# A long convolution joined with a two-layer MLP: token tiles of 512 columns in place of 390, a reordered second stage, and moved loads

## The chip, the cores and the metric

The kernel runs on one core of a Trainium2 chip. The metric is device time in microseconds (us) of one launch. The engines of the core are called PE (TensorE, with its weight loads as PEld), DVE (VectorE), ACT (ScalarE), POOL (GpSimd) and SP (SyncE, which here only issues DMAs).

## The reference

Two batches of 12480 tokens with 128 channels. The first part is a causal convolution of length 12480 by Fourier transforms, the second a two-layer MLP on each token:

```python
h_filt = (np.maximum(pos_emb @ w1, 0.0) @ w2) * window       # 12480 x 128
u = x * v                                                     # 2 x 12480 x 128
y = irfft(rfft(u, 2S) * rfft(h_filt, 2S))[:, :S]
t = (x * y).reshape(24960, 128)
h = t @ w_in                                                  # 128 -> 2048
out = np.maximum(0.01 * h, h) @ w_out                         # 2048 -> 128
```

## The kernel before

**The transform.** The convolution is a transform of length 98 x 128 in two stages. Stage 1 multiplies 98-row blocks by cosine tables (`ft`, `f1`) and stores to a scratch array in DRAM, stage 2 works on 25 chunks (`NCH`) of four rows `k` of that array: forward in 128 points, product with the spectrum of the filter, back in 128 points, store to `scr2`. A last stage (`front`) goes back over 98 points for one pair of column blocks at a time, `yp` (16 matmuls), and multiplies by `x`.

**Batch 0** does stage 1 and stage 2 ahead of the MLP, to about 350 us. The loop over its 25 chunks also makes the filter's spectrum and splits the MLP's weights. `load_b(c + 2)` fetches a chunk two turns ahead. In its last turn `load_tile(0)` issues, on SP's queue, the table `g` (300 KB), the tokens `xm` (192 KB and two small ones) and `cin` (the output of stage 2) of the first pair.

**The MLP** runs over 64 tiles, one for each pair, of `TOK` = 390 columns, and in each over 16 blocks `f` of the hidden layer (a step is one `f` of one tile). All operands are split into a high and a low part in fp32r, so a product is three matmuls. `m1(t, f)` is three matmuls into a PSUM tile `mh`; ACT makes `rh = relu(mh)` (L697), DVE makes `rl = relu(mh) - rh` (L698). `m2` of the step three before then adds three matmuls to `acc`; for f = 0 three more go first (L707 to L709). So a tile takes 16 x 6 + 3 = 99 matmuls of 390 columns. Between the steps the program emits, in an order written out by hand:

- `finish(t - 1)` at f = 2, 5, 7: copy of `acc`, four transposes into `op`, copy, store to the output;
- `join(t + 1)` at f = 6: two operations on POOL from `cin` to `cp`;
- `front(t + 1)` at f = 9 (transposes of `xm` into `xp`) and f = 12 (`yp`, then on DVE `zf`, on ACT `zh`, on POOL `zl`);
- the transform of batch 1, `conv1`, a generator cut into pieces at its yields. 32 pieces (`AHEAD`) go ahead of the MLP; the others are spread evenly, `(pieces - AHEAD) * slots // (SLOTS - 28)`, over the steps of batch 0, from the second step on.

In `conv1` stage 1 has 16 turns of 8 pieces. A turn fetches the next one's table and tokens (`fetch_a`, 600 KB and twice 384 KB), and POOL multiplies x by v (`mult_a`, L177). `fetch_a(4)` is issued in the turn c = 3 of the generator, within the 32 pieces, and once more by the line ahead of the MLP's loop (L744), into other buffers that nothing reads. Stage 2 (`conv1b`) takes about 15 pieces for a chunk: three-term products `up` (L131, 512 columns), `us` and `p1` on ACT, DVE and POOL, the back product `dp` of the chunk before and its copies, `ph` and `pl`, then `split` of the next chunk (`th` on ACT, `tl` on DVE L393).

Each engine works its instructions in program order. Each DMA queue issues in order, and an issue that waits holds those behind it.

Of the kernel before, what the change touches and what calls it, by code (L numbers as in the profile page):

```python
# [23 lines left out]
TOK = 4 * NA - 2  # L24


@with_exitstack
def tile_conv_mlp(ctx, tc, x, v, pos_emb, w1, w2, w_in, w_out, cf, cr, cg, cb, ci, cw, out):
# [128 lines left out]
    with tc.manual_schedule():  # L157
# [172 lines left out]
        N1 = HB // MC1  # L330
        PRE = 3
# [35 lines left out]
        def conv1b():  # L367
# [4 lines left out]
            def fetch_b(c):  # L372
                k0, n = chunk(c)
                t = pool.tile([128, KC, 2, D], F32, tag="bin1", name="bin1")
                nc.sync.dma_start(out=t[:, :n].rearrange("p k s d -> p k (s d)"), in_=scr1b[:, k0:k0 + n, :])
# [4 lines left out]
                got[c] = t  # L380
# [17 lines left out]
            for _ in range(5):  # L398
                yield
            yield from split(0)  # L400
            late, pins = None, {}
            for c in range(NCH + 1):
                if c + 1 < NCH:
                    fetch_b(c + 1)
# [3 lines left out]
                if c < NCH:  # L408
                    n = chunk(c)[1]
                    w = n * D  # L410
                    h, (th, tl) = hd.pop(c), parts.pop(c)
                    yield
                    up = psc["next"]()
                    for s in range(2):
                        three(up[s][:, :w].rearrange("p (k d) -> p k d", d=D), (mb_h[:, s], mb_l[:, s]),
                              (th[:, :n, s, :], tl[:, :n, s, :]))
                    yield

                    us = pool.tile([128, 2, 512], F32, tag="us", name="us", bufs=1)
                    p1 = pool.tile([128, 2, 512], F32, tag="p1", name="p1", bufs=1)  # L420
# [26 lines left out]
                if c + 1 < NCH:  # L447
                    yield from split(c + 1)
# [3 lines left out]
        pieces = N1 * (MC1 // 2) * 4 + 20 + 14 * NCH  # L452
# [7 lines left out]
        def load_tile(t):  # L460
# [8 lines left out]
            nc.sync.dma_start(out=xt[ROWS:, 0], in_=x[b, None, r0:r0 + 2, :])  # L469
            ci_t = mlp.tile([NA, 2, 2, 2, D], F32, tag="cin", name="cin")  # L470
# [3 lines left out]
            ld[t] = (ci_t, g, xt)  # L474
# [12 lines left out]
        with ExitStack() as st:  # L487
# [162 lines left out]
            evac(NCH - 1)  # L650
            ahead(A2)
# [11 lines left out]
        COLS = [(1, 0, 0, NA - 1), (1, 1, NA - 1, NA - 1), (0, 0, 2 * NA - 2, NA), (0, 1, 3 * NA - 2, NA)]  # L663

        def front(t):
# [15 lines left out]
            zh = sm.tile([128, TOK], F32R, tag="zh", name="zh")  # L681
            zl = sm.tile([128, TOK], F32R, tag="zl", name="zl")
            nc.vector.tensor_tensor(out=zf, in0=yp, in1=xs, op=ALU.mult)  # L683
            nc.scalar.copy(zh, zf)  # L684
            (nc.gpsimd if t else nc.vector).tensor_tensor(out=zl, in0=zf, in1=zh, op=ALU.subtract)  # L685
            z[t] = (zh, zl)

        def m1(t, f):
            zh, zl = z[t]
            hp = ps.tile([128, TOK], F32, tag="mh", name="mh", bufs=3)  # L690
# [4 lines left out]
            rh = sm.tile([128, TOK], F32R, tag="rh", name="rh", bufs=5)  # L695
            rl = sm.tile([128, TOK], F32R, tag="rl", name="rl", bufs=5)
# [4 lines left out]
        def m2(t, f, r):  # L701
            rh, rl = r
            if f == 0:
                zh, zl = z[t]
                ap = ps.tile([128, TOK], F32, tag="acc", name="acc", bufs=2)
                acc[t] = ap
# [3 lines left out]
            ap = acc[t]  # L710
# [4 lines left out]
        def finish(t):  # L715
            b, mp = divmod(t, NT)
            ot = sm.tile([128, TOK], F32, tag="ot", name="ot")
            nc.scalar.copy(ot, acc.pop(t))
            yield
            op = ps.tile([NA, 4, D], F32, tag="io", name="op")  # L720
            for p, m, at, n in COLS:
                nc.tensor.transpose(op[:, 2 * p + m, :], ot[:, at:at + NA], ident)  # L722
            os_ = sm.tile([NA, 2, 2, D], F32, tag="os", name="os")
            nc.scalar.copy(os_.rearrange("a p m d -> a (p m) d"), op)
            yield
            n = b * S
            dst = out[n:n + ROWS * NB, :].rearrange("(a p n) d -> a p n d", p=2, n=HB)
            for r in (slice(0, R0), slice(R0, ROWS)):
                nc.sync.dma_start(out=dst[r, :, 2 * mp:2 * mp + 2, :], in_=os_[r])
            r0 = n + ROWS * NB + 2 * mp  # L730
            nc.sync.dma_start(out=out[None, r0:r0 + 2, :], in_=os_[ROWS:, 0])

        total = B * NT
        SLOTS = NT * NF
        slots, done = 0, AHEAD
# [8 lines left out]
        fetch_a(4)  # L744
        pend = []
        fin = iter(())
        for t in range(total):
            if t + 1 < total and (t + 1) % NT:
                load_tile(t + 1)
            for f in range(NF):  # L750
                pend.append((t, f, m1(t, f)))
                if len(pend) > 3:
                    m2(*pend.pop(0))
                if f == 2 and t:
                    fin = finish(t - 1)
                if f in (2, 5, 7):
                    next(fin, None)
                if t + 1 == NT and f == 6:
                    run(conv)
                    load_tile(t + 1)  # L760
                if t + 1 < total:
                    if f == 6 and (t + 1) % NT:
                        join(t + 1)
                    if f == 9:
                        if (t + 1) % NT == 0:
                            join(t + 1)
                        frt = front(t + 1)
                    if f in (9, 12):
                        next(frt, None)
                if t < NT:  # L770
                    slots += 1
                    while done < AHEAD + (pieces - AHEAD) * slots // (SLOTS - 28):
# [4 lines left out]
        run(finish(total - 1))  # L777
# [68 lines left out]
```

## Time and profile before

| | us |
|---|---|
| median of 3 runs | 1787.03 |
| lowest, highest | 1785.88, 1787.2 |
| the profiled execution | 1786.13 |
| its span, first to last instruction | 1784.3 |
| PE busy in the span | 1709.8 |
| DVE, ACT, POOL busy | 952.3, 893.2, 559.3 |

The profile is one execution; its time and the median are 0.9 us apart. Busy time of PE counts overlapping matmuls once, and their ends are modelled, so how fast PE goes is read from the starts of matmuls, not from its busy share.

### The profile page before, as it was taken

Reading aid. Unit: us, or ns where it says so; the run is one execution under the profiler, and the core shown is the slowest. Engines: PE = TensorE matmul, PEld = TensorE weight load, DVE = VectorE, ACT = ScalarE, POOL = GpSimd, SP = SyncE. Lnnn points to the kernel's source line nnn. Section 1 sums busy time; section 2 is a strip of 40 time slices with the busy share of each in tenths; the row PEclk is TensorE's granted clock in tenths of the full one; section 3 lists DMA queues with packets and bytes.
Section 4 is the critical chain, followed back from the end, with each engine's and each line's share of the span. In section 5 each row is a group of like instructions: output and inputs, shape, how many; then the busy total and the mean of one; then the engine's idle time right before and its main releaser. Section 6 shows DMA issues by size and latency. Waiting matters only on the chain.

```text
span 1784.3 us, 29254 instructions
## 1 busy us (share of the span) xinstructions
PE 1709.8 (96%) x10620; PEld 1608.9 (90%) x10620; DVE 952.3 (53%) x1711; ACT 893.2 (50%) x1803; POOL 559.3 (31%) x427
## 2 busy tenths in 40 slices
PE   6788999889999999999999999999999999999998
PEld 5677555579999999999999999999999999999998
DVE  3566788744555555555555554444444444444444
ACT  1222444424445666666666666444444444444444
POOL 3453222122323555555544554211111112111120
PEclk8889999989999999999999999999999999999999
DMA  9898999796766465555555542222111221112210
GB/s 225 240 267 255 329 333 343 238 248 192 202 169 175 130 171 142 133 138 134 141 143 145 145 127 72 59 59 67 51 51 51 62 64 51 51 50 66 61 51 15
DMA packets 147708, 251.78 MB, mean 141 GB/s; under 512 B 10842, under 2 KB 96742, under 8 KB 144492
## 3 DMA queue, kind: packets, MB, share of 16 engines
q1 hardware_dynamic: 127420, 224.21, 45.3%
q10 hardware_dynamic: 20144, 25.69, 4.1%
q8 instruction: 84, 1.38, 0.3%
q14 instruction: 60, 0.49, 0.1%
HBM read 166.37 MB, written 83.43 MB: 140 GB/s over the span
## 4 chain that ended last, share of the span: by engine, by line
PE 79%; DMA 10%; DVE 6%; SPq 2%; issue 1%; ACT 1%; POOL 1%; ACTq 0%; POOLq 0%; DVEq 0%
PE mh L692 10%; PE mh L694 10%; PE acc L712 10%; PE acc L711 10%; PE mh L693 10%; PE acc L713 10%; PE yp L678 6%; PE cv L131 4%; PE cv L349 2%; DMA scr<-o 2%; DMA ft<-in_cf_dram 2%; PE op L722 2%; PE xp L670 1%; DVE ta L125 1%; PE up L117 1%
## 5 line engine op out<-in xcount | busy, mean ns | idle before, releaser
L698 DVE SCALAR_TENSOR_TENSOR rl<-mh,rh 128x390 fp32r<-128x390 f32 x1024 | 574.9, 564 | 616.6 <-ACT rh L697 614.8
L697 ACT ACTIVATE rh<-mh 128x390 fp32r<-128x390 f32 x1024 | 508.5, 498 | 386.9 <-PE mh L694 369.9
L692 PE MATMUL mh<-zh,w_in_h 128*128 128x390 f32 x1024 | 365.5, 357 | 0.0
L694 PE MATMUL mh<-zh,w_in_l 128*128 128x390 f32 x1024 | 349.9, 342 | 0.0
L693 PE MATMUL mh<-zl,w_in_h 128*128 128x390 f32 x1024 | 348.9, 341 | 0.0
L712 PE MATMUL acc<-rl,w_out_h 128*128 128x390 f32 x1024 | 348.4, 340 | 0.0
L711 PE MATMUL acc<-rh,w_out_h 128*128 128x390 f32 x1024 | 348.0, 340 | 0.0
L713 PE MATMUL acc<-rh,w_out_l 128*128 128x390 f32 x1024 | 347.8, 340 | 0.0
L685 POOL TENSOR_TENSOR zl<-zf,zh 128x390 fp32r<-128x390 f32 x63 | 65.0, 1032 | 706.3 <-ACT zh L684 699.0
L692 PEld LDWEIGHTS mh<-zh,w_in_h 128*128 128x128 f32 x1024 | 193.9, 189 | 2.2 <-DVE rl L698 0.2
L693 PEld LDWEIGHTS mh<-zl,w_in_h 128*128 128x128 f32 x1024 | 193.6, 189 | 2.1
L712 PEld LDWEIGHTS acc<-rl,w_out_h 128*128 128x128 f32 x1024 | 193.8, 189 | 0.0
L694 PEld LDWEIGHTS mh<-zh,w_in_l 128*128 128x128 f32 x1024 | 193.8, 189 | 0.0
L713 PEld LDWEIGHTS acc<-rh,w_out_l 128*128 128x128 f32 x1024 | 193.0, 188 | 0.0
L711 PEld LDWEIGHTS acc<-rh,w_out_h 128*128 128x128 f32 x1024 | 192.7, 188 | 0.0
L678 PEld LDWEIGHTS yp<-g,cp 98*128 98x128 f32 x1024 | 123.5, 192 | 0.5 <-issue 0.5
L678 PE MATMUL yp<-g,cp 98*128 98x97 f32 (+1 forms) x1024 | 123.2, 273 | 0.3 <-issue 0.3
L430 POOL TENSOR_TENSOR us<-us,hd 128x512 f32<-128x512 f32 (+1 forms) x50 | 63.6, 1273 | 145.8 <-ACT us L428 145.8
L684 ACT CAST zh<-zf 128x390 fp32r<-128x390 f32 x64 | 33.2, 519 | 149.3 <-DVE zf L683 149.3
L484 POOL TENSOR_TENSOR cp<-cin 98x512 f32<-98x512 f32 x63 | 88.3, 1402 | 0.0
L98 ACT COPY a1s<-a 98x384 f32<-98x384 f32 x64 | 30.7, 480 | 112.8 <-PE a L313 57.4
L483 POOL TENSOR_TENSOR cp<-cin 98x512 f32<-98x512 f32 x63 | 81.5, 1293 | 17.9 <-DMA cin<-scr 10.6
(127 smaller groups left out, 2102.1 us busy)
## 6 DMA issues: line engine op xcount, KB each, us to landing
cin<-scr SPq DMA_DIRECT2D x63, 392.0 KB
hd<-hspec SPq DMA_DIRECT2D x48, 512.0 KB
g<-in_cg_dram SPq DMA_DIRECT2D x64, 300.1 KB
scr<-o SPq DMA_DIRECT2D x32, 588.0 KB
bin<-scr SPq DMA_DIRECT2D x23, 768.0 KB
scr1b<-o SPq DMA_DIRECT2D x32, 392.0 KB
hspec<-hs ACTq DMA_DIRECT2D x48, 256.0 KB
scr<-ct ACTq DMA_DIRECT2D x24, 512.0 KB
```

Of the source, the lines that this page charges most:

```text
L131: nc.tensor.matmul(dst, u, w, start=(i == 0), stop=(i == 2))
L483: eng.tensor_tensor(out=o1, in0=c0, in1=c1, op=ALU.subtract)
L484: eng.tensor_tensor(out=o0, in0=c0, in1=c1, op=ALU.add)
L678: nc.tensor.matmul(yp[:, at:at + n], ci_t[:, r, m, p, :], g[:, r, p, m, :n], start=(r == 0), stop=(r == 1))
L692: nc.tensor.matmul(hp, w_in_h[:, fs], zh, start=True, stop=False)
L693: nc.tensor.matmul(hp, w_in_h[:, fs], zl, start=False, stop=False)
L694: nc.tensor.matmul(hp, w_in_l[:, fs], zh, start=False, stop=True)
L697: nc.scalar.activation(out=rh, in_=hp, func=AF.Relu)
L698: nc.vector.scalar_tensor_tensor(out=rl, in0=hp, scalar=0.0, in1=rh, op0=ALU.max, op1=ALU.subtract)
L711: nc.tensor.matmul(ap, w_out_h[:, f, :], rh, start=False, stop=False)
L712: nc.tensor.matmul(ap, w_out_h[:, f, :], rl, start=False, stop=False)
L713: nc.tensor.matmul(ap, w_out_l[:, f, :], rh, start=False, stop=(f == NF - 1))
```

## The change

The MLP runs over 50 tiles instead of 64: the first has 390 columns, then 23 of 512 and one of 314 end batch 0; batch 1 has 23 of 512 and two of 352. The pairs stay as they are (64 of 390 columns), so a pair's `zh`, `zl` and its output are written in up to two pieces (111 in all instead of 64), by `pieces_of`. `zh` and `zl` have three buffers instead of two, `rh` and `rl` four instead of five, and `m2` follows `m1` by two steps instead of three (`DEEP`). A table of steps (`ends`, `steps`) says when the front, join and load of each pair are emitted: the front's second half at least three steps ahead of the tile that needs it, join seven steps before that.

The pieces of batch 1's transform are paced by `pace`: none in the first 14 steps, stage 1 up to step 120, then stage 2 up to six steps ahead of step 375. In stage 2 `split` of the next chunk stands ahead of the back product, its load one chunk sooner, `us` and `p1` have two buffers, and 12 pieces instead of 5 lie between the first load and its use. `load_tile` is cut in `load_gx` and `load_c`: the g and x of pairs 0 and 1 are loaded in the turns of chunks 20 and 21, `cin` of pair 1 behind the last chunk. The second `fetch_a(4)` goes. (Pair 33's load is now issued twice, at steps 375 and 383.)

```diff
+        WAIT = 12
             fetch_b(0)
-            for _ in range(5):
+            fetch_h(0)
+            fetch_b(1)
+            for _ in range(WAIT):
                 yield
...
+                if c + 1 < NCH:
+                    yield from split(c + 1)
+                    fetch_b(c + 2)
                 if c:
                     wb = chunk(c - 1)[1] * D
...
-                if c + 1 < NCH:
-                    yield from split(c + 1)
...
+                if c in (NCH - 5, NCH - 4):
+                    load_gx(c - NCH + 5)
                 if c == NCH - 1:
-                    load_tile(0)
+                    load_c(0)
...
             evac(NCH - 1)
+            load_c(1)
             ahead(A2)
...
+        rest = S - TOK - (S - TOK) // WIDE * WIDE
+        widths = [TOK] + [WIDE] * ((S - TOK) // WIDE) + [rest]
+        left = S - (S // WIDE - 1) * WIDE
+        widths += [WIDE] * (S // WIDE - 1) + [left - left // 2, left // 2]
...
+            for k, a, c, n in pieces_of(t):
+                if k not in z:
+                    z[k] = [sm.tile([128, WIDE], F32R, tag=g, name=g, bufs=ZB) for g in ("zh", "zl")]
+                zh, zl = (i[:, a:a + n] for i in z[k])
+                nc.scalar.copy(zh, zf[:, c:c + n])
+                (nc.gpsimd if t else nc.vector).tensor_tensor(out=zl, in0=zf[:, c:c + n], in1=zh, op=ALU.subtract)
...
+        ZB, DEEP = 3, 2
+        first = [next(pieces_of(t))[0] for t in range(total)]
+        ends, e = {}, NTL * NF
+        for t in reversed(range(1, total)):
+            e = min(e - 8, first[t] * NF - 3)
+            ends[t] = e
...
+            at(ends[t] - 7, "join", t)
+            at(ends[t] - 3, "front", t)
+            at(ends[t], "front", t)
+            if t % NT == 0:
+                at(ends[t] - 14, "conv", t)
...
-        fetch_a(4)
+        STAGE1 = N1 * (MC1 // 2) * 4
+        FROM, TILL = 14, 120
+        def pace(i):
+            if i < TILL:
+                return AHEAD + (STAGE1 - AHEAD) * max(0, i - FROM) // (TILL - FROM)
+            return STAGE1 + (pieces - STAGE1) * (i + 1 - TILL) // (SLOTS - 6 - TILL)
...
-        for t in range(total):
+        for k in range(NTL):
             for f in range(NF):
-                if len(pend) > 3:
+                if len(pend) > DEEP:
                     m2(*pend.pop(0))
+                for s_ in steps.get(i, ()):
+                    do(*s_)
```

## Rows read from the trace of the kernel before

**Rows 1.** Windows: stretch, length, busy us (instructions) by engine, clock, DMA share, GB/s

```profile
360.00:391.00 31.00, 22.14 (x120) 21.35 (x119) 9.71 (x19) 8.71 (x17) 7.12 (x4) 0.83 0.90 249
...
575.00:1100.00 525.00, 524.32 (x3069) 507.91 (x3068) 283.20 (x478) 342.79 (x687) 267.03 (x211) 1.00 0.52 137
1100.00:1784.30 684.30, 679.45 (x4127) 675.98 (x4125) 322.22 (x570) 333.16 (x676) 115.64 (x99) 1.00 0.20 55
```

**Rows 2.** Groups by line: shapes, count, busy us, mean ns, idle before

```profile
L698 DVE SCALAR_TENSOR_TENSOR rl<-mh,rh 128x390 fp32r<-128x390 f32 x1024 | 574.9, 564 | 616.6 <-ACT rh L697 614.8
L697 ACT ACTIVATE rh<-mh 128x390 fp32r<-128x390 f32 x1024 | 508.5, 498 | 386.9 <-PE mh L694 369.9 <-ACT th L388 0.4
...
L426 DVE TENSOR_TENSOR p<-cv,hd 128x512 f32<-128x512 f32 (+1 forms) x50 | 34.1, 681 | 16.9 <-ACT us L425 13.3 <-DMA xm<-in_x_dram 1.0
```

**Rows 3.** Timeline of PE around 905 us: start us, length us, instruction

```profile
901.95 0.35 PE L692 MATMUL mh<-zh,w_in_h 128*128 128x390 f32 x1
...
907.30 0.33 PE L692 MATMUL mh<-zh,w_in_h 128*128 128x390 f32 x1
...
908.88 0.39 PE L131 MATMUL cv<-th,mb_h 128*128 128x512 f32 x1
...
910.25 0.34 PE L692 MATMUL mh<-zh,w_in_h 128*128 128x390 f32 x1
```

**Rows 4.** The chain that ended last, one of its six-matmul pieces: start, us

```profile
885.94 1.39 PE cv L131 x6
```

**Rows 5.** Timeline of PE where the MLP begins; in brackets idle before, and releaser

```profile
358.13 1.91 PE L349 MATMUL cv<-xv,ft 98*98 98x128 f32 x16
359.80 0.42 PE L692 MATMUL mh<-zh,w_in_h 128*128 128x390 f32 x1
...
366.31 3.13 PE L349 MATMUL cv<-xv,ft 98*98 98x128 f32 x16 [4.52 <-POOL xv L177]
369.10 0.68 PE L692 MATMUL mh<-zh,w_in_h 128*128 128x390 f32 x1
...
385.45 3.73 PE L349 MATMUL cv<-xv,ft 98*98 98x128 f32 x16 [4.34 <-POOL xv L177]
388.83 0.68 PE L692 MATMUL mh<-zh,w_in_h 128*128 128x390 f32 x1
```

**Rows 6.** Timeline of POOL over the same stretch

```profile
363.92 2.34 POOL L177 TENSOR_TENSOR xv<-xv,xv 98x1024 f32<-98x1024 f32 x1 [32.85 <-DMA xv<-in_v_dram]
...
385.35 1.26 POOL L483 TENSOR_TENSOR cp<-cin 98x512 f32<-98x512 f32 x1
```

**Rows 7.** Timeline of SP's queue, 290 to 400 us

```profile
314.51 0.34 SPq L495 DMA_DIRECT2D bin<-scr  x1
...
335.98 0.69 SPq L472 DMA_DIRECT2D cin<-scr  x1
...
362.54 0.33 SPq L164 DMA_DIRECT2D ft<-in_cf_dram  x1
```

**Rows 8.** Timeline of ACT's queue: stores of stage 2 of batch 0

```profile
333.05 0.37 ACTq L147 DMA_DIRECT2D scr<-ct  x1
...
348.92 0.37 ACTq L147 DMA_DIRECT2D scr<-ct  x1
```

**Rows 9.** Timeline of PE near the end of batch 0's chunks

```profile
323.76 1.04 PE L580 MATMUL ep<-mb,bin 128*64 128x128 f32 x16
```

**Rows 10.** Timeline of PE, batch 1's second stage: the last matmul of an `m1`

```profile
906.59 0.33 PE L694 MATMUL mh<-zh,w_in_l 128*128 128x390 f32 x1
```

**Rows 11.** Timeline of DVE, the same stretch

```profile
909.21 1.02 DVE L698 SCALAR_TENSOR_TENSOR rl<-mh,rh 128x390 fp32r<-128x390 f32 x2
```

**Rows 12.** Timeline of PE at a tile's end in batch 1's MLP

```profile
1511.10 1.92 PE L678 MATMUL yp<-g,cp 98*128 98x97 f32 x16
1512.81 0.42 PE L692 MATMUL mh<-zh,w_in_h 128*128 128x390 f32 x1
```

**Rows 13.** Timeline of POOL, the same stretch

```profile
1514.33 1.02 POOL L685 TENSOR_TENSOR zl<-zf,zh 128x390 fp32r<-128x390 f32 x1 [16.65 <-ACT zh L684]
```

More of the change, by code (lines that the diff above doesn't have):

```diff
@@ L24 @@
 TOK = 4 * NA - 2
+WIDE = 512
 @with_exitstack
@@ L473, in load_tile @@
                               in_=scr2[b][:k1, :, 2 * mp:2 * mp + 2, :].rearrange("k r m e -> k r (m e)"))
-            ld[t] = (ci_t, g, xt)
+            ld[t] = (ci_t, *ld[t][1:])
+        def load_tile(t):
+            load_gx(t)
+            load_c(t)
         def join(t):
@@ L680, in front, with m1 @@
             zf = sm.tile([128, TOK], F32, tag="zf", name="zf", bufs=1)
-            zh = sm.tile([128, TOK], F32R, tag="zh", name="zh")
-            zl = sm.tile([128, TOK], F32R, tag="zl", name="zl")
             nc.vector.tensor_tensor(out=zf, in0=yp, in1=xs, op=ALU.mult)
[L684 to L690, printed above, removed]
+            for k, a, c, n in pieces_of(t):
[4 more added lines that the diff above has]
+                (nc.gpsimd if t else nc.vector).tensor_tensor(out=zl, in0=zf[:, c:c + n], in1=zh, op=ALU.subtract)
+        def m1(k, f):
+            w = widths[k]
+            zh, zl = (i[:, :w] for i in z[k])
+            hp = ps.tile([128, WIDE], F32, tag="mh", name="mh", bufs=3)[:, :w]
             fs = slice(f * 128, f * 128 + 128)
@@ new lines, in tile_conv_mlp, with at @@
+        ZB, DEEP = 3, 2
[4 more added lines that the diff above has]
+            ends[t] = e
+        steps = {}
+        def at(i, what, t):
+            steps.setdefault(max(i, 0), []).append((what, t))
+        fronts = {}
+        for t in range(1, total):
+            at(ends[t] - 7, "join", t)
[3 more added lines that the diff above has]
+                at(ends[t] - 14, "conv", t)
+            elif t > 1:
+                at(ends[t - 2] + 1 if t > 2 and (t - 1) % NT else ends[t] - 14, "load", t)
@@ L736, in tile_conv_mlp, with do @@
+        def do(what, t):
+            if what == "conv":
+                run(conv)
+                load_tile(t)
+                load_tile(t + 1)
+            elif what == "load":
+                load_tile(t)
+            elif what == "join":
+                join(t)
+            elif t in fronts:
+                next(fronts.pop(t), None)
+            else:
+                fronts[t] = front(t)
+                next(fronts[t])
+        SLOTS = ends[NT] - 14
+        done = AHEAD
         frt = front(0)
@@ L743, in tile_conv_mlp @@
             next(conv)
-        fetch_a(4)
+        STAGE1 = N1 * (MC1 // 2) * 4
[4 more added lines that the diff above has]
+            return STAGE1 + (pieces - STAGE1) * (i + 1 - TILL) // (SLOTS - 6 - TILL)
         pend = []
         fin = iter(())
-        for t in range(total):
-            if t + 1 < total and (t + 1) % NT:
-                load_tile(t + 1)
+        for k in range(NTL):
             for f in range(NF):
-                pend.append((t, f, m1(t, f)))
-                if len(pend) > 3:
+                i = k * NF + f
+                pend.append((k, f, m1(k, f)))
+                if len(pend) > DEEP:
                     m2(*pend.pop(0))
-                if f == 2 and t:
-                    fin = finish(t - 1)
-                if f in (2, 5, 7):
-                    next(fin, None)
[L758 to L772, printed above, removed]
+                for s_ in steps.get(i, ()):
+                    do(*s_)
+                if f == DEEP - 1 and k:
+                    fin = finish(k - 1)
+                if f >= DEEP - 1 and (f - DEEP + 1) % 2 == 0:
+                    next(fin, None)
+                if i < SLOTS:
+                    while done < min(pieces, pace(i)):
                         next(conv, None)
```

97 lines of the change are left out of this document (60 added, 37 removed).

## The prediction, made before the changed kernel was run

> **What bounds the kernel now.** I read the windows first. From 575 us to the end PE has work practically without a break: 524.3 of 525.0 us while batch 1's transform runs in between, 679.5 of 684.3 us after it, and the granted clock is at its upper level, 2.4 GHz [rows 1]. DVE and ACT are at 50 to 65% there, DMA at 52% and then 20%. So three quarters of the span last as long as PE's own stream, and what counts is how closely its matmuls follow each other. The groups by line give the other engines' share of a step: 498 ns of ACT and 564 ns of DVE [rows 2].
>
> The timeline of PE gives the pitch. From 901.95 to 907.30 us lie five steps, 30 matmuls of 390 columns: 5.35 / 30 = 178.3 ns each. The six matmuls of 512 columns that follow take 910.25 - 908.88 = 1.37 us, 228.3 ns each [rows 3]. The chain of waits has other pieces of six; the one shown takes 1.39 us, 231.7 ns each [rows 4]. A line through 390 columns at 178.3 and 512 at 228.3 rises by 0.41 ns a column and leaves 18 ns that don't depend on the columns. The wider matmul is 28% longer and does 31% more.
>
> The exception is the begin of the MLP. Of 360 to 391 us PE is busy 22.1, and the clock's mean is 0.83 of 2.4 GHz [rows 1]: two pieces of the transform wait 4.52 and 4.34 us for POOL's product L177, and behind each wait the matmuls run at the lower level, 1.2 GHz [rows 5]. POOL itself waited 32.85 us for the tokens of `fetch_a(4)` [rows 6], and the same load stands in SP's queue a second time at 362.54 us [rows 7].
>
> **The change, part by part.**
>
> *Wide tiles.* Before: 64 x 99 = 6336 matmuls x 178.3 ns = 1129.7 us. After: 46 tiles of 512, 4554 matmuls, and four narrower ones. These come from the line above: 390 columns 178.3, 314 147.2, twice 352 162.7, together 651 ns x 99 = 64.4 us. For the 512 the rows leave 228.3 to 231.7 ns; I take 229.5, nearer to the run of six, which is measured from start to start in the midst of the narrow ones: 1045.1 us. Sum 1109.5, a gain of 20.2 us; the ends are 25.6 (228.3) and 10.1 (231.7). The pairs' own matmuls (`xp`, `yp`, `op`) and the transform's stay the same in number, so nothing else changes in PE's stream.
>
> The row shows 178.3 ns where the Trainium skill, "TensorE: Matmul & The Clock Gate", section "Back-to-back issue gap", gives columns / 2.4 + 2.5 ns when the clock is up, so 165 ns for 390 and 216 ns for 512. By it only 2.5 ns would be saved with each of the 1386 matmuls that go, 3.5 us instead of 20.2. This case's rows disagree with both figures by 12 to 13 ns, at both widths, so I go by the rows; the sum doesn't use the rule.
>
> *ACT and DVE.* A wide step costs ACT at most 498 x 512 / 390 = 654 ns and DVE 681 (an operation of 512 columns from PSUM [rows 2]) of 6 x 229.5 = 1377 ns of PE. The 47 further pieces of `zh` and `zl` lie on ACT and POOL, which are under 66% and 51% busy [rows 1]. Nothing of that bounds; they cost 0 while PE doesn't wait for them, which is the next point.
>
> *m2 two steps behind instead of three.* `rl` must be ready when `m2` reaches its second matmul. Before, between the end of an `m1` and there lay six trios and a matmul, 3.4 us; now four wide trios and one, 4 x 0.689 + 0.23 = 2.98 us. The worst `rl` that I found while the transform runs: `m1` ends at 906.92 [rows 10], the first of two `rl` that began at 909.21 with a joint 1.02 us ends about 509 ns later, at 909.72 [rows 11]: 2.8 us, and with wider operations (ACT 0.1, DVE 0.12) 3.0. Stage 2 also gets denser: 387 pieces over 249 steps, 1.55 a step, 1.13 per us of matmuls, against 466 over 484 steps, 0.90 per us. So the worst places just touch the limit. Between nothing and 249 steps x 0.04 = 10 us I take +2, nearer to nothing because DVE is busy in only 283 of the 525 us of that stretch [rows 1]. In batch 1, with no transform, there is room.
>
> *Front two steps ahead.* `zl` ends at 1515.35 [rows 13], 2.54 us behind the first matmul after `yp` [rows 12]. The next tile's first `zl` matmul comes two wide steps and 0.23 us behind it, about 3.0 us (before: three steps, 3.2). It holds; taken at 0, and where POOL or DVE is late it is part of the +2.
>
> *Begin of the MLP.* What is lost before: 4.52 + 4.34 us idle, and the two sets of 16 matmuls run 2.79 and 3.38 us instead of 1.67 [rows 5], 2.8 more: 11.7 us. After it no piece of the transform comes in the first 14 steps, so both waits for L177 go. But pair 1's `yp` now comes at step 5 instead of 12, and needs `join(1)`, which stands on POOL behind the product of `fetch_a(4)` (emitted within the 32 pieces). POOL gets that data at 363.92 [rows 6]. Now `load_c(1)` stands ahead of that fetch on SP's queue: it waits for chunk 24's store, issued at 348.92; the store at 333.05 released its load at 335.98, 2.6 us behind its issue [rows 8, 7], so this one is there at about 351.9, when SP comes to it. It costs some 0.9 us of issue and its 392 KB at 249 GB/s [rows 1] 1.6 us. Then L177 begins at about 366.4, ends at 368.7, and two operations of 1.26 us [rows 6] end at 371.2. PE begins the MLP at 359.80 [rows 5] and comes to `yp` after 33 matmuls and four transposes, 6.3 us: 366.1. So one new wait of 5.1 us, and the slow clock behind it, 1.1 as behind the first one. Gain 11.7 - 6.2 = 5.5 us. The bounds: 11.7 if `join(1)` is early enough, 1.5 if POOL's data come 4 us later than I think. The second fetch that goes takes 1.4 MB out of this stretch, behind the point that decides.
>
> *g and x in the turns of chunks 20 and 21.* Eight more DMA issues get between `load_b(22)` and `load_b(24)` on a queue that lies in its busiest stretch. `load_b(23)` is issued at 314.51 [rows 7] and first read at 323.76 [rows 9], 9.2 us later, so a delay of some us is covered; if each pair's loads hold SP for 3 us or more, PE waits. Bounds 0 and 6, taken +1: room is there, but not much. That nothing comes from their being gone later: `cin` at 335.98 waits for the store of 333.05 with or without them.
>
> *Stage 2 reordered, 12 pieces of waiting.* The cover of the first load grows; the stage's own stalls before are under 1 us (525.0 - 524.3 [rows 1]). Taken -0.5, between 0 and -1.
>
> *Turn to batch 1.* The last store goes at step 375, `cin(32)` behind it, `yp(32)` at 389: nine wide steps and five of 0.88 us, 16.8 us, for a store (2.6 us), a load of about the same and join (2.5). Cost 0; 3 us if the store lands late. The doubled load of pair 33 lies in the same room: 0.
>
> **Sum.** -20.2 - 5.5 - 0.5 + 2 + 1 = -23.2 against the profiled execution's 1786.1 us: 1762.9. The runs' median lies 0.9 above that execution, so 1763.8, rounded 1764 us.
>
> **The rivals.**
> - *The begin is clear.* `join(1)` comes early because fetch and store land sooner than I count; then 6.2 us more are gained: 1758 us. For it: DMA is not full at every moment there. Against: POOL's order is fixed, and L177 stands first.
> - *The shorter distance decides.* If `rl` is late on average and not only at the worst places, PE waits in each of the 249 steps of stage 2; every 0.1 us on average costs 24.9. From 0.093 us the gain of 23.2 is gone, and with 0.15 us it is 1778 + 23 = 1801, slower. For it: 2.8 us measured against 2.98 of room, and more pieces per us. Against: 2.8 is the end of the distribution, and ACT at 65%. In between, 0.04 to 0.08 us, lie 1772 to 1784.
> - *The pitch doesn't follow the rows.* If the fixed part of a matmul were 2.5 ns as in the rule named above, the gain of the tiles would be 3.5 us: 1781. Against it stand both widths in the rows.
> - *The loads at chunks 20 and 21 hold up the stage.* If SP needs 3 us longer for each pair, chunks 23 and 24 come late, up to 6 us: 1769.
>
> **How the numbers follow.** Forecast, 1754 to 1772: 0.60. Clear begin: 0.12. Shorter distance: 0.19, of which 0.12 still faster, 0.03 within 0.2%, 0.04 slower. Pitch: 0.04. Loads: 0.05. The measurement tells about 0.2%, 3.6 us, from no change. So faster 0.92, within 0.03, slower 0.05. The range goes from 1751 (the clear begin with 228.3 ns would lie below) to 1778 (most of the shorter distance and the pitch lie above), which leaves out about 0.18.
>
> **What would show it.** Six starts of `m1` and `m2` in a wide tile 1.37 to 1.39 us apart; 4950 MLP matmuls. No wait for L177 at the MLP's begin, but one of PE at `yp` of pair 1, released by POOL's join. In stage 2 few waits of PE on `rl`, each under 0.5 us; the windows of batch 1 full. The load of chunk 23 about 2 us later than 314.5 us, and its first reader not much later than 323.8 us. I am wrong if the wide matmuls are over 232 ns apart, or if PE's idle time in stage 2 is over 10 us.

## The result and the profile after

The changed kernel takes 1767.24 us (median of four runs, 1763.23 to 1771.21) against 1786.45 of the kernel before on the same chip: 0.9897 of its time, 95% interval 0.9866 to 0.9927. The forecast was 1764 us, 1751 to 1778. The profiled execution took 1764.67 us with a span of 1762.9, 21.4 less than before.

Two marks divide this. The first `m1` of the MLP begins at 366.2 us, before at 359.8 [rows 5], so what lies ahead of it became 6.4 us longer. From there to the start of the MLP's last matmul it takes 1390.9 us, before 1418.7: 27.8 less. The forecast had no gain ahead of the MLP, only its +1 us for the moved loads, and -24.2 behind the first `m1`.

The windows of the kernel after, with the columns of [rows 1]:

```profile
356.00:366.20 10.20, 10.10 (x52) 10.13 (x53) 4.91 (x8) 2.14 (x4) 0.00 (x0) 0.54 0.91 254
360.00:391.00 31.00, 31.00 (x183) 30.36 (x183) 14.65 (x26) 13.01 (x27) 9.46 (x8) 0.89 0.57 160
575.00:1100.00 525.00, 523.16 (x2564) 431.81 (x2563) 285.04 (x403) 335.15 (x648) 279.60 (x234) 1.00 0.56 149
1100.00:1762.90 662.90, 658.06 (x3372) 557.87 (x3370) 298.64 (x451) 310.78 (x601) 112.13 (x118) 1.00 0.19 53
```

PE is full again from 575 us on, and now also from 360 to 391, where it was busy for 22.1 us before [rows 1]. In the first stretch, the 10.2 us ahead of the MLP, it is busy too, but at a mean clock of 0.54, which is almost all the time its lower level, 1.2 GHz.

The pitch of the wide matmuls, from the timeline of PE in batch 1's MLP, the first of an `m1` and what follows four steps later:

```profile
1500.12 0.39 PE L730 MATMUL mh<-zh,w_in_h 128*128 128x512 f32 x1
...
1505.62 0.50 PE L706 MATMUL xp<-ident,xm 97*128 97x97 f32 x4
```

Between these two starts lie 24 matmuls: 5.50 / 24 = 229.2 ns; the forecast took 229.5. For 390 columns it was 178.3 [rows 3]. The other engines' shares of a step, by line and shape:

```profile
L736 DVE SCALAR_TENSOR_TENSOR rl<-mh,rh 128x512 fp32r<-128x512 f32 x736 | 507.1, 690 | 580.6 <-ACT rh L735 577.8
...
L735 ACT ACTIVATE rh<-mh 128x512 fp32r<-128x512 f32 x736 | 439.9, 599 | 350.3 <-PE mh L732 326.3 <-DVE rl L736 12.2 <-DVE usp L434 3.2
```

ACT takes 599 ns and DVE 690 (estimated: at most 654, and 681) of the 1375 ns that PE needs for a step. In stage 2 of batch 1 the sum of PE's waits, by the view of waits from 575 to 1100 us (us in total, times, longest):

```profile
PE acc L751 <- DVE rl L736: 1.4, 6, 0.3
PE acc L750 <- ACT rh L735: 0.2, 1, 0.2
```

Now the begin of the MLP, in the timelines of PE, DVE, POOL and SP's queue, in this order:

```profile
356.10 0.53 PE L706 MATMUL xp<-ident,xm 97*128 97x97 f32 x4 [3.35 <-issue]
356.46 3.35 PE L351 MATMUL cv<-xv,ft 98*98 98x128 f32 x16
359.60 3.57 PE L714 MATMUL yp<-g,cp 98*128 98x97 f32 x16
362.96 3.62 PE L351 MATMUL cv<-xv,ft 98*98 98x128 f32 x16
366.24 0.68 PE L730 MATMUL mh<-zh,w_in_h 128*128 128x390 f32 x1
...
373.12 1.92 PE L714 MATMUL yp<-g,cp 98*128 98x97 f32 x16
```

```profile
326.42 0.29 DVE L81 TENSOR_SCALAR fa<-wi 128x256 uint32<-128x256 uint32 x1 [6.88 <-DMA wi<-in_moe_w_in_dram]
...
354.71 0.69 DVE L101 TENSOR_TENSOR o<-hp,a1s 98x512 f32<-98x512 f32 x1 [4.48 <-DMA scr1b<-o]
...
361.57 0.69 DVE L101 TENSOR_TENSOR o<-cv,a1s 98x512 f32<-98x512 f32 x1 [2.36 <-DMA scr1b<-o]
```

```profile
368.03 2.40 POOL L178 TENSOR_TENSOR xv<-xv,xv 98x1024 f32<-98x1024 f32 x1 [33.25 <-PE mh L732]
370.39 1.29 POOL L500 TENSOR_TENSOR cp<-cin 98x512 f32<-98x512 f32 x1
371.64 1.29 POOL L501 TENSOR_TENSOR cp<-cin 98x512 f32<-98x512 f32 x1
```

```profile
312.38 0.36 SPq L512 DMA_DIRECT2D bin<-scr  x1
...
316.43 0.61 SPq L478 DMA_DIRECT2D xm<-in_x_dram  x1
321.95 0.35 SPq L524 DMA_DIRECT2D wi<-in_moe_w_in_dram  x1
322.40 0.67 SPq L525 DMA_DIRECT2D wo<-in_moe_w_out_dram  x1
323.15 0.48 SPq L512 DMA_DIRECT2D bin<-scr  x1
...
354.12 0.90 SPq L485 DMA_DIRECT2D cin<-scr  x1
355.11 1.00 SPq L364 DMA_DIRECT2D scr1b<-o  x2
```

Both waits for POOL's product (now L178) are gone. The wait that was forecast in their place, of PE at `yp` of pair 1, is not there: the join ends at 372.93, and PE comes to that `yp` only at 373.12, 6.9 us after its first `m1`. It comes there later because the MLP begins later, and the rows show three links of that. SP issues the last weights (`wi`) at 321.95, behind the moved loads of g and x, and DVE stands 6.88 us waiting for them, with stage 2's products behind it in its order. Of that delay 4.9 us lie between the end of the last moved issue (317.04) and `wi`; why SP stood still there isn't shown. (In the kernel before a pause of 5.3 us stands ahead of `xm`, behind `wi`.) There `wi` was issued sooner, and DVE had no wait for it:

```profile
314.95 0.39 SPq L507 DMA_DIRECT2D wi<-in_moe_w_in_dram  x1
```

Then DVE waits 4.48 and 2.36 us for a buffer `o` of stage 1, until its store to `scr1b` has landed. And behind PE's pause of 3.35 us ahead of `xp` the clock is at the lower level: sixteen matmuls that take 1.9 us at the upper one take 3.35 to 3.62.

### The profile page after: what moved, and what is told of

Its sections match the earlier page's. It is cut to its first block, busy times and chain, and to the rows that moved or that the text cites. A ratio compares the mean times of both kernels' runs of the same rounds, so it can differ in the third digit from the quotient of the medians.

```text
span 1762.9 us, 25710 instructions
## 1 busy us (share of the span) xinstructions
PE 1693.3 (96%) x9234; PEld 1399.2 (79%) x9234; DVE 929.5 (53%) x1487; ACT 861.4 (49%) x1673; POOL 566.5 (32%) x474
## 4 chain that ended last, share of the span: by engine, by line
PE 82%; DMA 10%; DVE 3%; ACT 1%; SPq 1%; issue 1%; POOL 1%; ACTq 0%; DVEq 0%; POOLq 0%
PE mh L730 10%; PE acc L751 10%; PE acc L752 10%; PE mh L732 10%; PE acc L750 10%; PE mh L731 10%; PE yp L714 6%; PE cv L132 4%; DMA xt<-in_x_dram 3%; PE cv L351 3%; DMA hspec<-hs 2%; PE op L774 2%; DMA ft<-in_cf_dram 1%; PE xp L706 1%; PE up L118 1%; PE dp L139 1%
## 5 line engine op out<-in xcount | busy, mean ns | idle before, releaser
L736 DVE SCALAR_TENSOR_TENSOR rl<-mh,rh 128x512 fp32r<-128x512 f32 (+3 forms) x800 | 540.2, 677 | 613.7 <-ACT rh L735 610.8
L735 ACT ACTIVATE rh<-mh 128x512 fp32r<-128x512 f32 (+3 forms) x800 | 469.5, 588 | 372.7 <-PE mh L732 348.2
L730 PE MATMUL mh<-zh,w_in_h 128*128 128x512 f32 (+3 forms) x800 | 327.1, 409 | 0.0
L751 PE MATMUL acc<-rl,w_out_h 128*128 128x512 f32 (+3 forms) x800 | 309.5, 387 | 1.4 <-DVE rl L736 1.4
L750 PE MATMUL acc<-rh,w_out_h 128*128 128x512 f32 (+3 forms) x800 | 310.4, 388 | 0.2 <-ACT rh L735 0.2
L732 PE MATMUL mh<-zh,w_in_l 128*128 128x512 f32 (+3 forms) x800 | 309.9, 387 | 0.0
L752 PE MATMUL acc<-rh,w_out_l 128*128 128x512 f32 (+3 forms) x800 | 309.8, 387 | 0.0
L731 PE MATMUL mh<-zl,w_in_h 128*128 128x512 f32 (+3 forms) x800 | 308.8, 386 | 0.0
L723 POOL TENSOR_TENSOR zl<-zf,zh 128x390 fp32r<-128x390 f32 (+24 forms) x110 | 67.9, 631 | 700.7 <-ACT zh L722 700.3
L438 POOL TENSOR_TENSOR usp<-usp,hd 128x512 f32<-128x512 f32 (+1 forms) x50 | 65.3, 1306 | 59.5 <-ACT usp L436 42.1
```

What stands on the lines that cost most here:

```text
L730: nc.tensor.matmul(hp, w_in_h[:, fs], zh, start=True, stop=False)
L731: nc.tensor.matmul(hp, w_in_h[:, fs], zl, start=False, stop=False)
L732: nc.tensor.matmul(hp, w_in_l[:, fs], zh, start=False, stop=True)
L735: nc.scalar.activation(out=rh, in_=hp, func=AF.Relu)
L736: nc.vector.scalar_tensor_tensor(out=rl, in0=hp, scalar=0.0, in1=rh, op0=ALU.max, op1=ALU.subtract)
L750: nc.tensor.matmul(ap, w_out_h[:, f, :], rh, start=False, stop=False)
```

## The experiments

Each row is a kernel on its own; times are medians, the ratio is to the kernel before on the same chip, and the last two columns are read from its trace: the start of the first `m1`, and the distance from there to the start of the MLP's last matmul.

| | us | ratio [95%] | first m1 | to the last |
|---|---|---|---|---|
| before | 1787.03 | | 359.8 | 1418.7 |
| changed | 1767.24 | 0.9897 [0.9866, 0.9927] | 366.2 | 1390.9 |
| again | 1767.88 | 0.9910 [0.9886, 0.9933] | 362.4 | 1391.8 |
| narrow | 1799.01 | 1.0091 [1.0073, 1.0109] | 366.9 | 1425.5 |
| narrow3 | 1785.53 | 1.0000 [0.9985, 1.0014] | 367.0 | 1410.2 |
| deep3 | 1765.79 | 0.9904 [0.9887, 0.9920] | 368.7 | 1389.9 |
| no_double | 1777.21 | 0.9963 [0.9948, 0.9977] | 357.9 | 1411.4 |
| from0 | 1770.87 | 0.9924 [0.9902, 0.9945] | 369.3 | 1393.3 |
| old_order | 1795.99 | 1.0069 [1.0055, 1.0082] | 367.1 | 1421.9 |
| late_gx | 1763.33 | 0.9890 [0.9872, 0.9909] | 366.6 | 1391.5 |
| c1_later | 1767.21 | 0.9899 [0.9876, 0.9922] | 369.6 | 1391.5 |
| store_early | 1766.33 | 0.9900 [0.9887, 0.9914] | 366.5 | 1391.8 |
| store_join | 1765.98 | 0.9901 [0.9886, 0.9917] | 364.8 | 1390.7 |
| best3 | 1757.59 | 0.9834 [0.9816, 0.9852] | 360.8 | 1390.8 |

**again**: the changed kernel itself.

> The changed kernel itself, once more, so that the three kernels beside it can be compared with it on the same chip. Expected: 1764 to 1768 us, about 0.99 of the time before, the first m1 at about 366 us of its trace, the six waits of PE for rl in stage 2 of 0.3 to 0.5 us each.

The second execution of the same program has its first `m1` 3.8 us sooner than the first one. So the begin varies by some us from execution to execution, and differences of it between two traces are read below over shorter distances. Here PE came to `yp` of pair 1 early enough to meet the forecast wait, though only 0.43 us of it:

```profile
369.82 2.36 PE L714 MATMUL yp<-g,cp 98*128 98x97 f32 x16 [0.43 <-POOL cp L500]
```

**narrow** and **narrow3**: the width, against deep3 below. Both have `m2` three steps behind, as deep3 has, and the pace stretched to the greater number of steps; the line with `NF - 4` is in narrow3 alone.

```diff
-WIDE = 512
+WIDE = 390
...
-        widths = [TOK] + [WIDE] * ((S - TOK) // WIDE) + [rest]
+        widths = [TOK] * total
...
-        widths += [WIDE] * (S // WIDE - 1) + [left - left // 2, left // 2]
...
-        ZB, DEEP = 3, 2
+        ZB, DEEP = 3, 3
...
-            e = min(e - 8, first[t] * NF - 3)
+            e = min(e - 8, first[t] * NF - 4)
...
-        FROM, TILL = 14, 120
+        FROM, TILL = 14, 153
```

> The changed kernel with all 64 tiles at 390 columns and m2 three steps behind, everything else as in the change (loads, order of stage 2, pace stretched so that stage 1 ends at step 153). Against the run deep3 it differs in the width alone. Theory (15 to 16 ns of each matmul don't depend on its columns): 6336 matmuls at 178 ns against 4950, 20 us longer than deep3, 1784 to 1787. Rival (only 2.5 ns of a matmul are fixed, and the gain came from the begin of the MLP): 3.5 us longer than deep3, 1768 to 1771.

> All 64 tiles at 390 columns as before the change, with all the rest of the change, m2 three steps behind, and the front's second half four narrow steps ahead of its tile (the kernel labelled narrow had it three ahead and paid a wait of PE for zl at each tile). Theory (a matmul of 512 columns takes 229.5 ns, one of 390 178.3, so 6336 matmuls of 390 cost 20 us more than 4950 in the widths of the change): 18 to 24 us longer than the kernel labelled deep3, so 1784 to 1790 us. Rival by a fixed part of 2.5 ns a matmul: 3 to 4 us longer, 1769 us. Other rival (the pieces of zh, zl and the fronts at odd places cost something that only wide tiles have): under 15 us longer.

narrow missed by more than ten us, and its trace says why. At the first step of a new tile, in 48 of the 63, the matmul on `zl` comes late:

```profile
1505.02 0.34 PE L729 MATMUL mh<-zh,w_in_h 128*128 128x390 f32 x1
1505.39 0.45 PE L730 MATMUL mh<-zl,w_in_h 128*128 128x390 f32 x1
```

0.37 us lie between the two starts in place of 0.18, and the next one follows 0.29 us later instead of 0.18: 0.3 us, which over 48 tile starts makes about 14; narrow is 13.5 us over narrow3, and 15.3 by the marks. Two narrow steps and a matmul, 2.32 us, are less than the 2.54 us that `zl` needs [rows 12, 13], two wide ones and a matmul, 2.98 us, are more. With one step more, narrow3 has no such place and measures the width: 1785.53 - 1765.79 = 19.7 us over deep3, and 20.3 us from the first `m1` to the last matmul; the kernel before has 1784.4 and 1784.5 us on the two chips. The forecast was 20.2 us for the tiles. The two rivals, 3 to 4 us and under 15 us, are out.

**deep3**: `m2` three steps behind, as before the change.

```diff
-        ZB, DEEP = 3, 2
+        ZB, DEEP = 3, 3
```

> The changed kernel with m2 three steps behind m1 instead of two (DEEP = 3, rh and rl five buffers). Its trace had six places in the second stage of batch 1's transform where the second matmul of m2 came 0.56 to 0.74 us behind the first instead of 0.23, 2.7 us together. Theory (the shorter distance costs only these places): they go, and the time is 1 to 3 us below the changed kernel's 1767, so 1764 to 1766. Rival (the whole stage loses time to the shorter distance, up to 10 us): about 1757. Rival (other waits take their place): 1767.

Its waits of PE from 575 to 1100 us, by the same view as above:

```profile
PE mh L730 <- DVE rl L736: 2.1, 3, 1.4
```

The six waits for `rl` go, and three others come, of `m1` for a buffer `mh` that DVE's same operation still reads. So with more distance DVE's late operations hold PE up one place further on, and the time is 1 to 2 us lower, which is within the noise.

**no_double**: the kernel before, without its line L744.

```diff
-        fetch_a(4)
```

> The kernel before without the second fetch_a(4), nothing else. Theory (its 1.4 MB and seven DMA issues stand ahead of the load of turn 5, whose product PE waited for at 380.8 to 385.5 us): that wait and the slow clock behind it go, 5 to 7 us: 1779 to 1782. Rival (the transfer is hidden, the wait comes from the pace of the pieces): 1785 to 1787.

The second wait for POOL's product, 4.34 us at 385.45 [rows 5], is gone with its slow matmuls; the first one stays, 4.26 us. The time falls by about 7 us, and by the marks 1418.7 - 1411.4 = 7.3 us. Its rest to the changed kernel, 1411.4 - 1390.9 = 20.5, is about the width; that the first wait, 4.26 us and gone in the changed kernel, doesn't show in it is taken up below.

**from0**: the pieces of the transform from the MLP's first step on.

```diff
-        FROM, TILL = 14, 120
+        FROM, TILL = 0, 120
```

> The changed kernel with batch 1's transform paced from step 0 of the MLP on in place of step 14 (FROM = 0), nothing else. Theory (the gap of 14 steps is what took away the first wait for POOL's product L177, since POOL has the data only at about 366 us): the wait comes back, one of 2 to 5 us behind the first steps with slow matmuls behind it, and the time is 2 to 8 us longer than the changed kernel's. Rival (the later begin of the MLP, 366 us in place of 360, has outrun that wait anyway): no wait for L177 over 1 us, the time the same within 1.5 us.

```profile
375.30 1.99 PE L351 MATMUL cv<-xv,ft 98*98 98x128 f32 x16 [0.67 <-POOL xv L178]
```

The wait comes back with 0.67 us of the former 4.52, as the rival had it; the distance to the last matmul is 1.5 to 2.4 us longer, and the time 3.0 us over the run again, as the theory had it, though within the noise of the two. But the rival's reason, the later begin, isn't what the rows show:

```profile
372.86 2.38 POOL L178 TENSOR_TENSOR xv<-xv,xv 98x1024 f32<-98x1024 f32 x1 [35.45 <-DVE rl L736]
```

POOL's product ends at 375.24, 6.0 us behind the first `m1` (369.25); before the change it ended at 366.26, 6.5 us behind it [rows 5, 6]. So the product comes later together with the MLP. What shortens the wait is that PE comes to it later: 5.4 us behind its first `m1`, after 21 matmuls of the MLP and four transposes, the first eight of them at a mean clock of 0.50; before it was 2.0 us, after nine matmuls at 1.00.

**old_order**: the split of the next chunk behind the back product again, all else as changed.

```diff
-                if c + 1 < NCH:
-                    yield from split(c + 1)
-                    fetch_b(c + 2)
                 if c:
                     wb = chunk(c - 1)[1] * D
...
+                if c + 1 < NCH:
+                    yield from split(c + 1)
+                    fetch_b(c + 2)
             late()
```

> The changed kernel with the split of the next chunk put back behind the back product in batch 1's second stage, and the load with it; us and p1 keep their two buffers and the first load its cover. The prediction gave the new order 0.5 us (0 to 1). Theory: the time the same within 2 us, PE's idle time from 575 to 1100 us below 3 us as with the new order. Rival (at the new pace of 1.5 pieces a step the old order can't keep up, so the reorder is what makes the pace possible): waits of PE for th, tl or the load in most of the 25 chunks, 5 us or more longer.

The rival holds, with a price that I had not thought of: 28 us over the changed kernel, slower than the kernel before. PE's waits from 575 to 1100 us:

```profile
PE cv L132 <- ACT usp L436: 11.9, 13, 1.2
PE cv L132 <- DVE tl L399: 7.1, 10, 1.2
PE acc L750 <- ACT rh L735: 3.6, 1, 3.6
```

In the old order the back product follows the forward one at once and waits for the PSUM buffers `cv` that ACT is still reading (L436), and the next forward product then waits for a split that has only just been made. That is 13 and 10 waits over the chunks of that stretch, 22.6 us with the third line; from 575 to 700 us the mean clock is 0.97 besides. The kernel before had the same order and 0.7 us of idle time there [rows 1], at 0.90 pieces per us instead of 1.13. That the pace makes this difference is argued: no run has the old order with the wide tiles and `m2` two steps behind at the old pace.

**late_gx**: g and x of the first two pairs back to the places that they had with `cin`.

```diff
-                if c in (NCH - 5, NCH - 4):
-                    load_gx(c - NCH + 5)
                 if c == NCH - 1:
-                    load_c(0)
+                    load_tile(0)
...
-            load_c(1)
+            load_tile(1)
```

> The changed kernel with the loads of g and x of pairs 0 and 1 back behind the chunks (pair 0's in the turn of chunk 24, pair 1's with its cin). Theory (the early loads held up the last load of the weights by 7 us on SP's queue, and with it chunk 23 and the MLP's begin, 366.2 instead of 359.8 us): up of chunk 24 comes at about 337 instead of 340.6 us and the MLP begins at 360 to 363 us, but then pair 1's yp waits for POOL's join, which stands behind the product of the tokens and ends at about 372 us, so the time is within 2 us of the changed kernel: 1765 to 1769. Rival (the whole delay is given back): 1761. Rival (early g and x are what lets the MLP begin without waits): 3 us or more slower, 1770 and above.

The last weights are issued sooner again, and so comes chunk 24's `up` product, at 338.37 us:

```profile
317.31 0.39 SPq L524 DMA_DIRECT2D wi<-in_moe_w_in_dram  x1
```

But then pair 1's loads stand ahead of the store L364 on SP's queue, and DVE's second wait for `o` grows from 2.36 us to 6.15:

```profile
363.57 0.69 DVE L101 TENSOR_TENSOR o<-cv,a1s 98x512 f32<-98x512 f32 x1 [6.15 <-DMA scr1b<-o]
```

The first `m1` is where it was. What one place gave, the next one took.

**c1_later**: the load of pair 1's `cin` behind four more pieces.

```diff
-            load_c(1)
             ahead(A2)
+            load_c(1)
```

> The changed kernel with the load of cin of pair 1 moved behind the next four pieces of the transform, so that the store of stage 1's second turn (scr1b, L364) goes ahead of it on SP's queue. Theory (the store held up behind that load keeps o's buffer, DVE waits for it, PE waits for DVE, and its clock falls to the lower level): the store is issued near 352 us in place of 355.1, DVE's wait of 4.48 us at 354.7 shrinks by 2 to 3 us, the first m1 comes 2 to 6 us sooner than 366.2, and the time is 2 to 6 us under the changed kernel's; some of it may come back as a wait of PE for join(1) at yp of pair 1. Rival (the begin is late because chunks 23 and 24 are late, and the store only fills that time): the first m1 within 1 us of 366.2, the time the same.

A miss. The second wait for `o` is gone, but the first one is there with 4.96 us, and behind PE's pause of 3.83 us the clock falls, to a mean of 0.55 up to the first `m1`:

```profile
358.46 0.69 DVE L101 TENSOR_TENSOR o<-hp,a1s 98x512 f32<-98x512 f32 x1 [4.96 <-DMA scr1b<-o]
```

I had taken the wrong store. That wait is for the store of stage 1's first turn. The turn itself is done before batch 0's chunks begin, but `conv1` issues its store only when the generator is resumed, behind the last chunks: at 348.08 in the changed kernel.

**store_early**: one piece more in the turn of chunk 12, one less at the end, so the generator is resumed early and stores.

```diff
                 if c in MULT:
                     mult_a(1 + MULT.index(c))
+                if c == 12:
+                    next(conv)
...
-        for _ in range(4 * A5):
+        for _ in range(4 * A5 - 1):
```

> The changed kernel with one piece of the transform moved from the last ones ahead of the MLP to the turn of chunk 12, so that the stores of stage 1's first two turns (scr1b, L364) are issued as soon as their turns are done; before, the first one waited till the next piece, behind all chunks. Theory (what holds up the begin is DVE's wait for the buffer o, whose store was issued only 4 us earlier): the waits of DVE for scr1b<-o of 2 to 5 us near 352 to 358 us go, PE's wait of 3 us ahead of xp of pair 0 too, the clock doesn't fall to its lower level there, and from xp of pair 0 to the first m1 it takes 6 us in place of 8 to 12. But then yp of pair 1 comes before join(1), which stands on POOL behind L178, and PE waits there for 2 to 7 us, as the prediction had it: time 0 to 5 us under the changed kernel's. Rival (the wait for o only covers something else that is as late): the first m1 no sooner, the time the same.

Both waits of DVE for `o` are gone, and so is PE's pause ahead of `xp` (0.30 us). In its place PE waits 1.64 us at `yp` of pair 0 for `join(0)`, whose last rows of `cin` now stand behind the store on SP's queue, and at that place the clock falls. From `xp` to the first `m1` it takes 10.2 us, not 6. The forecast wait at `yp` of pair 1 doesn't come, for the same reason as in the changed kernel.

**store_join**: as store_early, and pair 1's join ahead of L178. The edit against store_early:

```diff
-            at(ends[t] - 7, "join", t)
+            if t > 1:
+                at(ends[t] - 7, "join", t)
...
         join(0)
+        join(1)
```

> As the kernel labelled store_early, and join of pair 1 is emitted right behind that of pair 0, ahead of the product L178 of the fourth fetch on POOL. Theory: no wait of PE for cp of pair 1, none for o; the first m1 near 356 to 360 us and no idle time of PE over 1 us behind it; 3 to 8 us under the kernel labelled store_early if that one waits at yp of pair 1, so 1756 to 1762 us. Rival (POOL isn't what is late there, but the load of cin of pair 1): the wait stays, released by a DMA, and the time is that of store_early.

No wait for `cp` of pair 1, but in time no different from store_early, since that one didn't wait there either. The pair of traces shows something else. The same PE instructions run up to `yp` of pair 0, with the same 1.64 us of idle time ahead of it:

```profile
360.30 3.16 PE L716 MATMUL yp<-g,cp 98*128 98x97 f32 x16 [1.64 <-DVE cp L500]
```

```profile
361.32 2.00 PE L716 MATMUL yp<-g,cp 98*128 98x97 f32 x16 [1.64 <-DVE cp L500]
```

The first of these is store_early, the second store_join. In the one the granted clock from there to the first `m1` is 0.55, in the other 1.00.

**best3**: store_join with three steps' distance, and g and x of both pairs in the last chunk's turn, behind all that the chunks need. The edit against store_join:

```diff
-                if c in (NCH - 5, NCH - 4):
-                    load_gx(c - NCH + 5)
                 if c == NCH - 1:
+                    load_gx(0)
+                    load_gx(1)
                     load_c(0)
...
-        ZB, DEEP = 3, 2
+        ZB, DEEP = 3, 3
```

> What the runs so far point to, put together: the kernel labelled store_join (early stores of stage 1, join of pair 1 first), m2 three steps behind, and the g and x of pairs 0 and 1 both loaded in the last chunk's turn, behind the loads that the chunks and the weights need. Theory (in the ten traces with g and x in the turns of chunks 20 and 21 the up product of chunk 24 begins at 338.8 to 345.0 us, in the three without at 335.5 to 338.4): chunk 24's up product near 337 us, xp of pair 0 near 351 us, no wait of PE for o, cin or cp over 1 us, the first m1 at 356 to 360 us with the clock at its upper level, and 1390 us from there to the last matmul: a span of 1752 to 1757 us, 6 to 12 us under the changed kernel's time. Rival (the begin is as late for another reason, or pair 1's cin or xm arrives late and PE waits at its yp): within 3 us of the kernel labelled store_join, 1763 to 1767 us.

It is the fastest kernel: 1757.59 us, 29.7 under the kernel before and 10.3 under the run again, and its interval lies clear of the changed kernel's. Not all came as told: chunk 24's `up` product stands at 341.02, not near 337, since this execution was already late at chunk 20. The rows of PE from there on, the `up` products of chunks 20 and 24 and the begin:

```profile
312.19 3.53 PE L118 MATMUL up<-bin,mb 128*64 128x512 f32 x8 [2.18 <-DVE ta L126]
...
341.02 1.16 PE L118 MATMUL up<-bin,mb 128*64 128x256 f32 x8 [2.78 <-DVE ta L126]
...
353.44 0.53 PE L708 MATMUL xp<-ident,xm 97*128 97x97 f32 x4 [0.30 <-PE up L351]
...
357.31 2.00 PE L716 MATMUL yp<-g,cp 98*128 98x97 f32 x16 [1.60 <-ACT a1s L99]
...
360.81 0.42 PE L732 MATMUL mh<-zh,w_in_h 128*128 128x390 f32 x1
```

The same two rows of the changed kernel:

```profile
304.77 2.96 PE L118 MATMUL up<-bin,mb 128*64 128x512 f32 x8 [2.18 <-DVE ta L126]
...
340.63 1.16 PE L118 MATMUL up<-bin,mb 128*64 128x256 f32 x8 [1.61 <-DVE ta L126]
```

The same rows of the kernel before:

```profile
309.41 1.94 PE L117 MATMUL up<-bin,mb 128*64 128x512 f32 x8 [2.17 <-DVE ta L125]
...
336.92 1.98 PE L117 MATMUL up<-bin,mb 128*64 128x256 f32 x8 [3.99 <-DVE ta L125]
```

From chunk 20 to chunk 24 best3 takes 28.8 us, the changed kernel 35.9. (I go by this distance, since the start of chunk 20 itself lies between 304.8 and 312.2 us from trace to trace.) Over all traces that distance is 27.5, 28.8, 28.4 and 28.8 us in the four without loads in the turns of chunks 20 and 21 (before, no_double, late_gx, best3), and 34.0 to 36.0, mean 35.2, in the ten with them. In each of the ten DVE waits 5.5 to 8.4 us for `wi`, in the four it doesn't wait for it. From chunk 24 to the first `m1` it is 19.8 us in best3 and 25.6 in the changed kernel. best3's PE waits 1.60 us at `yp` of pair 0 and 0.94 us at the first `zl`, and the clock stays at the upper level.

## Why the prediction was right, and where not

**The wide tiles** were sized right: -20.2 forecast, -19.7 by the times and -20.3 by the marks (narrow3 against deep3). The pitch came from rows of matmuls of the same operand types, and the line through two widths held: 229.2 ns measured, 229.5 taken. The rule in the Trainium skill, "TensorE: Matmul & The Clock Gate", "Back-to-back issue gap", with 2.5 ns a matmul, would have left 3.5 us, as an estimate; narrow3 against deep3 speaks against it for this kernel. That section calls the rule the gap of an isolated matmul, and for a stream of matmuls gives about 131 ns at 512 columns in its place, which the 229.2 ns of this kernel don't bear out either.

**m2 two steps behind** cost about what was taken, +2: the six waits are 1.4 us by the view of waits, and 2.7 us by the starts of the matmuls, which come 0.56 to 0.74 us behind the one before in place of 0.23; deep3, where other waits come instead, gains 2 us at most. The rival in which the shorter distance decides is out. **The front** holds with the room that was forecast, and narrow shows that the room was needed: with 0.2 us too little, most tile starts pay 0.3 us. **ACT and DVE** and **the turn to batch 1** cost nothing: the view of waits has no wait of PE from 1100 to 1160 us.

**The begin of the MLP** had the right parts, but most of them met at other times than the forecast had. The waits for L177 are gone, as the step said. One of them, with what followed it, was worth 7.3 us and belonged to the second `fetch_a(4)` alone (no_double). The other was to go by the 14 empty steps; from0 shows that without them only 0.67 us of it is left, since PE comes to the product 5.4 us behind its first `m1` in place of 2.0.

The forecast new wait at `yp` of pair 1 is 0.43 us in one execution and none in the other, instead of 5.1. POOL's times were forecast right: in the run again the join's two operations end at 369.76 and 370.99, forecast was 371.2. But the first `m1` came 2.6 us (again) and 6.4 us later than the forecast had it, and `yp` starts in again when the first of the two operations has ended.

Of the 5.6 us (4.52 and 1.1) that the first wait and its slow matmuls cost before, little is left in the sum: narrow3 has neither wait, but from its first `m1` to the last matmul it is only 1.2 us shorter than no_double. By the starts of PE's matmuls two new losses stand against it. In narrow3's stage 2 six `m1` come 0.40 to 1.51 us behind the matmul before them in place of 0.18, 3.1 us together (the view of waits counts 2.1); and its first nine matmuls of the MLP, at a mean clock of 0.55, take 3.4 us, no_double's 1.8. Together that is 4.7 us, about the 4.4 that are missing.

**The step that failed** is that of the loads of g and x in the turns of chunks 20 and 21. I took +1 us, between 0 and 6; the traces show 35.2 - 28.4 = 6.8 us, past the bound. I had looked at the next `load_b` on the queue and its reader, and there was room for that one. The load that was late was another one, issued behind the moved ones in the turn of chunk 21: the last weights, at 321.95 in place of 314.95 us, and they have DVE for a reader, which stands ahead of stage 2's products in DVE's order. The rival "the loads hold up the stage" thus happened in full. That the forecast held all the same is in part luck: the later begin made the new wait at `yp` vanish, and the 6.2 us forecast for that wait and its slow matmuls nearly equal the 6.4 us by which the MLP began later.

**The reordered stage 2** was sized at -0.5 from its own stalls before the change. As a difference to the kernel before that is nearly right: PE's waits for the transform's own operands in stage 2 are 0.6 us before and none after. As the worth of the edit within this change it is wrong: it is 28 us (old_order). The step looked at the stage of the old kernel only, and the same diff changed its pace, the width of the tiles and the distance of `m2`.

**The sum.** By the marks: -20.3 for the width, -7.3 for the second fetch and -0.2 for all else, in which the first wait's end and the new losses nearly cancel, make -27.8; the begin gives back 6.4; together -21.4, against -23.2 forecast for the profiled execution.

## What to carry to other kernels

Where an edit is judged by the stalls that it removes, judge it within the rest of the change, and not in the old kernel alone: here the old order of stage 2 cost under 1 us before the change and 28 us within it. A load that is moved forward on a queue is paid by whatever was issued behind it there, so list all of these with their first readers, not only the next one of the stage in view. And a gain ahead of a bound engine arrives only when the last of the chain's waits goes: here late_gx and store_early each changed nothing that could be told from the changed kernel, and best3, which has both ideas (with the early join and with `m2` three steps behind, which by themselves gave nothing clear of the noise), gave 10 us.

## What the runs showed of the hardware

I had not expected that the clock of PE would part two executions with the same instructions and the same pauses. Ahead of `yp` of pair 0, store_early and store_join show the same 1.64 us of idle time behind a stretch with the clock at its upper level and 8.36 and 8.39 of 10.3 us busy, and only one of them falls, as the windows show (store_early, then store_join):

```profile
350.00:360.30 10.30, 8.36 (x74) 7.47 (x72) 6.00 (x10) 3.67 (x8) 0.00 (x0) 1.00 0.52 158
360.30:366.50 6.20, 6.20 (x32) 6.20 (x33) 2.78 (x5) 0.52 (x1) 0.00 (x0) 0.55 0.92 243
```

```profile
351.00:361.30 10.30, 8.39 (x73) 7.48 (x72) 5.97 (x10) 3.70 (x8) 0.00 (x0) 1.00 0.55 176
361.30:364.80 3.50, 3.48 (x32) 3.50 (x32) 2.53 (x5) 0.52 (x1) 0.26 (x1) 1.00 0.91 245
```

The same 32 matmuls take 6.2 us in the one and 3.5 in the other. So a pause of PE ahead of a dense stretch costs its own length and, here in one of two executions, 2.7 us more; a forecast from one execution should carry that as a spread.
